# Last token block of a bilinear transformer layer: how the down stages are dealt between the products

## The chip, the cores and the metric

The kernel runs on one of the eight cores of a Trainium2 chip. The core's engines run side by side and meet at semaphores: TensorE (PE in the profile; its weight loads, PEld, overlap its matmuls), VectorE (DVE), ScalarE (ACT), GpSimd (POOL) and SyncE (SP), which here issues the transfers between memory and the on-chip buffers. The metric is the device time of one execution in microseconds (us); lower is better.

## The reference

One pre-norm layer on 2048 tokens of width 576: attention with 32 query heads of 18 and one shared key and value head, then a feed-forward part without a nonlinearity, the product of two projections to 4608, brought back by a third.

```python
h  = x + attention(layernorm(x)) @ wo          # 32 heads, one k and one v
xn = layernorm(h)
g  = xn @ w_gate                               # 576 -> 4608
u  = xn @ w_up                                 # 576 -> 4608
out = h + (g * u) @ w_down                     # 4608 -> 576
```

All is float32, and the change touches the last part of the feed-forward alone.

## The kernel before

The tokens are worked in four blocks of 512 (`TB`, `NB`). Blocks 0 to 2 have attention work mixed into their feed-forward. The last block (`b = 3`) has none left and is worked by `last_block`. The 4608 hidden columns are 18 pairs (`NC`, loop variable `p`) of 256. A float32 matrix product is made of three matmuls, high by high, high by low and low by high, of operands that were split before: ScalarE casts the high part (`high`), VectorE subtracts it to get the low part (`low`).

**Products.** For each pair, gate and up come from a seven-product scheme (the Winograd form of Strassen's) instead of eight: `product(i)` with i = 7p to 7p + 6 is 12 matmuls of 256 columns, and four of the seven are followed by a `tail` of 4 matmuls for the last 64 input columns. The results lie in four banks of the accumulator memory: `a` (`gs0` or `gs1`, by turns over the pairs), `b_` (`gs2`) and `c` (`gs3`). The bank `a` takes products 0, 3, 5 and 6 of a pair, and between two of them something must have read it: after product 5 that is VectorE's sum `gu22`. GpSimd multiplies gate by up (`both_halves`), giving the quarters a11, a21, a22 of the hidden tile; the last one, a12, comes from product 6 through ScalarE (`g`) and VectorE. Quarters and their sums S are split into an operand tile A with seven places. There are three such tiles in rotation (`AB`; one lies in the tile called `room`, two in the one called `XW`).

**Down stages.** The way back to 576 columns, `down_pairs`, takes two pairs at a time, also by seven products (`QUAD`). It is a generator of 14 steps: for each of the seven down weights (`wdo`, 288 KB each, from the `wd_dram` tensor, ten buffers) a step for each half t of 128 tokens. A step is three matmuls of 288 columns for each of the pairs, so six, into one half of the tile `yq` of that t (two banks), and then an add of that half to the residual h: on VectorE (L1112), or for four of the 14 steps (`ASIDE`) by a ScalarE copy (L1116) and a GpSimd add (L1117). The step of the second t also starts the loads of the next down weights. `last_block` takes steps of the generator D between the products by `go()`. While pairs 2 and 3 are multiplied, D holds pairs 0 and 1, and so on; while pairs 0 and 1 are multiplied, D holds the last pair of the block before, whose `down` has a plain form (L855): eight steps of six matmuls, one per token quarter s and half n of the columns, added by VectorE (n = 0) or by ScalarE and GpSimd (n = 1), and a store of the output rows after each s.

In the kernel before a pair takes seven steps: one after products 0, 1, 2, 3 and 6, two after product 5, none after product 4. So pairs 14 and 15 end after product 6 of pair 17, and behind it come pair 16 alone (14 steps of three matmuls) and pair 17 (eight plain groups of six, L1269, the first four into the banks `gs0`, `gs2`, `gs3`, `gs1`, the last four into two tiles `ye`, each used twice in a row), with an add (L1273) per group and a store of 288 KB per token quarter.

**Order.** The order on each engine is the order in which the code is written: no scheduler moves anything. An engine waits where its instruction's operand is not ready, and everything behind it on that engine waits too. `feed(i)` follows each product with the work for later ones: the low part of product i + 3's weights on VectorE, the high part of i + 4's on ScalarE, the load for i + 8 on SyncE.

Of the kernel before, what the change touches and what calls it, by code (L numbers as in the profile page):

```python
# [26 lines left out]
P = 128  # L27
S, D, H, DH, F = 2048, 576, 32, 18, 4608
TB = 512
NB = S // TB  # L30
# [4 lines left out]
NC = NF // 2  # L35
HT = TB // 2
HD = D // 2
# [20 lines left out]
class Block:  # L58
# [784 lines left out]
    def down(self, b, pair):  # L843

        pe, dve, act, sp, pool = self.pe, self.dve, self.act, self.sp, self.nc.gpsimd
        h = self.h[b]
        W = [self.wdo.pop((b, pair, j), None) for j in range(7)]
        if pair == NC - 1:
            ys = {}

            def part(s, n, i):

                ms = [(self.A[:, k, 2 * i + s // 2], W[(1, 0, 2, 3)[2 * i + n]][:, l]) for k, l in ((0, 0), (0, 1), (1, 0))]
                for j, (m, k) in enumerate(ms):
                    pe.matmul(ys[s, n][:, :HD], m[:, s % 2 * P:(s % 2 + 1) * P], k, start=(i == j == 0), stop=(i == 1 and j == 2))  # L855

            def add(s, n):
                hs, y = h[:, s, n * HD:(n + 1) * HD], ys.pop((s, n))[:, :HD]
                if n:
                    z = self.tmp[:, self.n_tmp % 5]  # L860
                    self.n_tmp += 1
                    act.copy(z, y)
                    pool.tensor_tensor(hs, hs, z, ALU.add)
                else:
                    dve.tensor_tensor(hs, hs, y, ALU.add)

            for s in range(NQ):
                if b == NB - 2:
                    e = self.ps_s(f"y{b}_{pair}_{s}")
                for n in range(2):  # L870
                    ys[s, n] = e[:, n] if b == NB - 2 else self.ps_y(2 * s + n, f"y{b}_{pair}_{s}_{n}")
                    part(s, n, 0)
                    part(s, n, 1)
                    add(s, n)
                    yield
                sp.dma_start(self.out[b * TB + s * P: b * TB + (s + 1) * P, :], h[:, s, :])
            return
        c, a = self.ps_f(f"y{b}_{pair}_2"), self.ps_f(f"y{b}_{pair}_0")
        banks = [a, self.ps_m(f"y{b}_{pair}_1"), c]
        for i, (t, bank, (x, w), first, (s, n), on_dve) in enumerate(STAGES):  # L880
            y = banks[bank]
# [6 lines left out]
            hs = h[:, t + 2 * s, n * HD:(n + 1) * HD]  # L888
# [234 lines left out]
    def last_block(self, ahead, D):  # L1123

        pe, act, dve, pool = self.pe, self.act, self.dve, self.nc.gpsimd
        b = NB - 1
# [25 lines left out]
        def both_halves(to, gu):  # L1152
            pool.tensor_tensor(to, gu[:, 0:HT], gu[:, HT:], ALU.mult)
# [7 lines left out]
        def low(i, src, n=1):  # L1161
            dve.tensor_tensor(A[:, 1, i:i + n], wide(src), f32(A[:, 0, i:i + n]), ALU.subtract)

        def go(n=1):
            for _ in range(n):
                next(D, None)

        late = []
        for p in range(NC):
            end = p == NC - 1  # L1170
            A = self.AB[(p + 1) % 3]
            if p % 2 == 0 and p:
                drain(D)
                D = self.down_pairs(b, (p - 2, p - 1))
# [4 lines left out]

            product(i, a, True)  # L1180
            act.copy(c1, a)
            go()
# [6 lines left out]
            go()  # L1189
# [5 lines left out]
            go()  # L1195
# [5 lines left out]
            go()  # L1201
# [5 lines left out]
            both_halves(a21, gu12)  # L1207
            self.feed(i + 4)

            product(i + 5, a)  # L1210
# [9 lines left out]
            go(2)  # L1220
            if p == 1:
                drain(D)
                if self.n_wd < len(self.wd_list):
# [4 lines left out]
            tail(1, 2, a)  # L1228
            if end:
                high(5, a22)  # L1230
                go()
                low(5, a22)
            else:
                low(5, S[:, 2])
                dve.tensor_tensor(S[:, 0], a21, a22, ALU.add)
                high(2, a22)
                dve.tensor_tensor(S[:, 1], S[:, 0], a11, ALU.subtract)
                go()
                high(3, S[:, 0:2], 2)
                low(2, a22)  # L1240
            self.feed(i + 6)
# [13 lines left out]
                low(6, S[:, 3])  # L1255
            del hf, a11, a21, a12, a22, g
        drain(D)
        drain(self.down_pairs(b, (NC - 2,)))
        W = [self.wdo.pop((b, NC - 1, j)) for j in range(4)]
        k = 0  # L1260
        for s in (2, 3, 0, 1):
            for n in range(2):
                if k in (4, 6):
                    e = self.ps_s(f"ye{k}")
                y = (gs[0], b_, c, gs[1])[k] if k < 4 else e[:, k % 2]
                for x in range(2):
                    at = ((0, 4), (6, 5))[x][s // 2]
                    for j, (m, l) in enumerate(((0, 0), (0, 1), (1, 0))):
                        pe.matmul(y[:, :HD], A[:, m, at, s % 2 * P:(s % 2 + 1) * P], W[(1, 0, 2, 3)[2 * x + n]][:, l],  # L1269
                                  start=(x == j == 0), stop=(x == 1 and j == 2))  # L1270
                k += 1
                hs = h[:, s, n * HD:(n + 1) * HD]
                dve.tensor_tensor(hs, hs, y[:, :HD], ALU.add)  # L1273
            self.sp.dma_start(self.out[b * TB + s * P: b * TB + (s + 1) * P, :], h[:, s, :])

    def load_x(self, b):
        h = self.h[b] = self.hp.tile([P, NQ, D], F32, tag="h", name=f"h{b}")
# [88 lines left out]
    def run(self):  # L1366
# [160 lines left out]
def drain(gen):  # L1527
    for _ in gen:
        pass
# [85 lines left out]
```

## Time and profile before

| | us |
|---|---|
| median of 3 runs (2296.19 to 2300.3) | 2297.45 |
| the profiled execution | 2295.16 |
| its span, first to last instruction | 2293.4 |
| TensorE busy in it | 2252.8 |
| stage of pair 16 behind the products | 10.9 |
| stage of pair 17 behind it | 8.3 |

The last block begins near 1957 us and its last product ends at 2269.55. In rows of the profile the name before the arrow is the tile written, those behind it are the tiles read, with partitions x elements. A row of the timeline begins with the start and the length in us, ends with the number of instructions merged into it, and in square brackets with how long the engine had stood idle before and who released it. PEld rows are the better clock of TensorE's pace, since the ends of matmuls are modelled.

### The profile page before, as it was taken

What the parts mean: (1) busy time and instruction counts of PE and PEld (TensorE: products, weight loads), DVE (VectorE), ACT (ScalarE), POOL (GpSimd) and SP (SyncE); (2) the same over time, 40 slices, a digit from 0 to 9 for tenths busy, and PEclk for the clock granted to TensorE, in tenths of its full rate; (3) what the DMA queues carried; (4) which work ended last, traced back from release to release, by engine and by line L of the source; (5) the groups of instructions that cost most, each with busy time, mean ns of one, the idle gap of its engine ahead of it and who ended that gap; (6) DMA issues with size and microseconds to landing.
All of it is one profiled execution on the core that took longest, in us unless ns stands there. A gap on an engine that the chain in (4) does not pass through costs nothing.

```text
span 2293.4 us, 46345 instructions
## 1 busy us (share of the span) xinstructions
PE 2252.8 (98%) x17958; PEld 1631.7 (71%) x17958; DVE 1268.2 (55%) x2209; ACT 1509.5 (66%) x2046; POOL 713.0 (31%) x826
## 2 busy tenths in 40 slices
PE   7999999999999999999999999999999999999998
PEld 5333335777677777777777777777777788999998
DVE  7555635444445446444545445444444477788786
ACT  6888877767676765767776766577676623555553
POOL 5445401333233333323333333322222233222222
PEclk9999999999999999999999999999999999999999
DMA  5779843555455555644455554644343345677774
GB/s 173 247 255 300 285 167 97 168 156 161 153 171 167 168 171 155 211 143 162 155 175 161 170 172 157 212 146 130 125 130 107 121 154 161 209 241 235 242 239 149
DMA packets 199127, 407.05 MB, mean 177 GB/s; under 512 B 21326, under 2 KB 52942, under 8 KB 198902
## 3 DMA queue, kind: packets, MB, share of 16 engines
q1 hardware_dynamic: 196165, 392.78, 53.3%
q0 software_dynamic: 2736, 11.26, 1.6%
q8 instruction: 143, 2.34, 0.4%
q14 instruction: 83, 0.67, 0.1%
HBM read 317.27 MB, written 74.55 MB: 171 GB/s over the span
## 4 chain that ended last, share of the span: by engine, by line
PE 83%; DVE 3%; ACT 1%; issue 0%; DMA 0%; SPq 0%; DVEq 0%; ACTq 0%
PE pg L932 21%; PE acc L611 15%; PE y L884 13%; PE s L606 9%; PE gs L1143 8%; PE pu L932 5%; PE yq L1108 4%; PE yo L736 3%; PE gu L932 2%; PE gs L1150 2%; PE y L855 1%; ACT P L607 0%; DVE hf L961 0%; DVE ws L93 0%; ACT room L92 0%
## 5 line engine op out<-in xcount | busy, mean ns | idle before, releaser
L607 ACT ACTIVATE P<-s 128x1024 f32<-128x1024 f32 x1024 | 1026.2, 1027 | 280.9 <-PE s L606 199.6
L932 PE MATMUL pu<-X,ws 64*128 64x512 f32 x2565 | 693.4, 389 | 0.0
L932 PE MATMUL pg<-X,ws 64*128 64x512 f32 x2565 | 692.8, 389 | 0.0
L932 PEld LDWEIGHTS pg<-X,ws 64*128 64x128 f32 x2565 | 475.3, 185 | 67.5 <-DMA wsum<-in_wgs_dram 0.8
L611 PE MATMUL acc<-P,V 128*32 128x512 f32 x4096 | 491.3, 599 | 0.7 <-ACT P L607 0.6
L932 PEld LDWEIGHTS pu<-X,ws 64*128 64x128 f32 x2565 | 472.6, 185 | 11.5
L606 PE MATMUL s<-q,kT 56*128 56x512 f32 x2048 | 438.5, 422 | 6.0 <-ACT P L607 3.1
L895 POOL TENSOR_TENSOR h<-h,tmp 128x288 f32<-128x288 f32 x306 | 238.7, 808 | 613.6 <-ACT tmp L894 612.6
L606 PEld LDWEIGHTS s<-q,kT 56*128 56x128 f32 x2048 | 197.2, 184 | 206.6 <-ACT P L607 120.5
L884 PEld LDWEIGHTS y<-wdo,room 128*128 128x128 f32 x2142 | 289.5, 188 | 45.1 <-issue 34.5
L884 PE MATMUL y<-wdo,room 128*128 128x288 f32 x2142 | 303.0, 300 | 3.6 <-DVE h L890 3.6
L611 PEld LDWEIGHTS acc<-P,V 128*32 128x32 f32 x4096 | 114.5, 109 | 247.2 <-issue 240.1
L890 DVE TENSOR_TENSOR h<-h,y 128x288 f32<-128x288 f32 x408 | 176.1, 453 | 199.3 <-PE y L884 199.1
L894 ACT COPY tmp<-y 128x288 f32<-128x288 f32 x306 | 122.3, 400 | 240.7 <-PE y L884 224.4
L961 DVE TENSOR_TENSOR hf<-pu,g 128x512 f32<-128x512 f32 x95 | 65.8, 692 | 301.7 <-ACT g L957 300.4
L92 POOL CAST ws<-wr 128x1152 fp32r<-128x1152 f32 x108 | 126.3, 1170 | 324.4 <-PE pu L932 235.1
L93 DVE TENSOR_TENSOR ws<-wr,ws 128x1152 fp32r<-128x1152 f32 x108 | 182.5, 1690 | 62.6 <-POOL ws L92 62.6
L1091 POOL TENSOR_TENSOR wsum<-wsum,wsum 128x512 f32<-128x512 f32 x72 | 99.0, 1376 | 139.9 <-DMA wsum<-in_wgs_dram 139.9
L93 DVE TENSOR_TENSOR room<-S,room 128x1024 fp32r<-128x1024 f32 x51 | 62.7, 1229 | 133.9 <-ACT room L92 133.9
L1108 PE MATMUL yq<-wdo,XW 128*128 128x288 f32 x504 | 88.2, 302 | 1.9 <-DVE h L1112 1.5
L737 DVE TENSOR_TENSOR h<-h,yo 128x288 f32<-128x288 f32 x160 | 65.1, 452 | 33.3 <-PE yo L736 33.2
L932 PE MATMUL gu<-X,ws 64*128 64x512 f32 x702 | 81.9, 389 | 0.0
(245 smaller groups left out, 2622.1 us busy)
## 6 DMA issues: line engine op xcount, KB each, us to landing
wdo<-wd_dram SPq DMA_DIRECT2D x492, 288.0 KB
wr<-in_wgu_dram SPq DMA_DIRECT2D x108, 576.0 KB
wsum<-in_wgs_dram SPq DMA_DIRECT2D x108, 256.0 KB
wd_dram<-wd_room SPq DMA_DIRECT2D x20, 1008.0 KB
wsum_dram<-wsum SPq DMA_DIRECT2D x72, 256.0 KB
raw<-wsum_dram SPq DMA_DIRECT2D x72, 256.0 KB
q<-q_dram SPq DMA_DIRECT2D x64, 216.0 KB
raw<-in_wgs_dram SPq DMA_DIRECT2D x54, 256.0 KB
```

The source lines that it names most:

```text
L92: (copy or self.cast)(hi, src)
L93: self.dve.tensor_tensor(lo, src, f32(hi), ALU.subtract)
L606: self.pe.matmul(s_[:, i], self.kT[o:o + 56, t * P:(t + 1) * P], q[o:o + 56, pr], start=True, stop=True)
L607: self.act.activation(p_, s_, AF.Exp, scale=SCALE)
L611: self.pe.matmul(acc[32 * j:32 * j + 32, :], self.V[:, t, :], Ps[j // 2][:, j % 2, :], start=(t == 0), stop=(t == NT - 1), skip_group_chec ...
L884: pe.matmul(y[:, :HD], m[:, t * P:(t + 1) * P], k, start=(first and j == 0), stop=(j == 2), skip_group_check=True)
L890: dve.tensor_tensor(hs, hs, y[:, :HD], ALU.add)
L894: act.copy(z, y[:, :HD])
L895: pool.tensor_tensor(hs, hs, z, ALU.add)
L932: pe.matmul(ps, w[o:o + 64, wk, c], X[o:o + 64, xk, c], start=(j == 0), stop=(j == 26))
L1108: pe.matmul(y[:, :HD], A[:, k, x, t * P:(t + 1) * P], v[:, l], start=(first and z == j == 0), stop=(z == len(pairs) - 1 and j == 2), skip_ ...
L1143: pe.matmul(bank[:, g * HT:(g + 1) * HT], W[:, wk, c, g], X[:, 2 * xk + c], start=(first and g == c == wk == xk == 0), stop=(c == 1 and wk ...
```

## The change

Four things change in the code.

The number of steps after each product is now read from a table, `DEALT`: a row for pairs 0 and 1, one for pairs 2 to 15 (as before, seven a pair), one for pairs 16 and 17. In pairs 16 and 17 it is two after every product. Pair 16 thus takes all 14 steps of pairs 14 and 15, and pair 17 all 14 steps of pair 16, whose generator is now made at the start of pair 17. Behind the products only pair 17's eight groups are left. In pairs 0 and 1 it is one step after products 1, 2, 3 and 5.

The plain steps of pairs 0 and 1 use two tiles made once, one for each half n of the columns, in place of one tile for each s; the half of the tile is s mod 2. Likewise the last four groups go by turns to two `ye` tiles.

The last token quarter is stored in two halves of its columns, the first as soon as it is added.

```diff
+            if b == NB - 2:
+                e = [self.ps_s(f"y{b}_{pair}_{n}") for n in range(2)]
             for s in range(NQ):
-                if b == NB - 2:
-                    e = self.ps_s(f"y{b}_{pair}_{s}")
                 for n in range(2):
-                    ys[s, n] = e[:, n] if b == NB - 2 else self.ps_y(2 * s + n, f"y{b}_{pair}_{s}_{n}")
+                    ys[s, n] = e[n][:, s % 2] if b == NB - 2 else self.ps_y(2 * s + n, f"y{b}_{pair}_{s}_{n}")
...
-        def go(n=1):
-            for _ in range(n):
+        def go(k):
+            for _ in range(DEALT[0 if p < 2 else 2 if p > NC - 3 else 1][k]):
                 next(D, None)
...
-            if p % 2 == 0 and p:
+            if p % 2 == 0 and p or end:
                 drain(D)
-                D = self.down_pairs(b, (p - 2, p - 1))
+                D = self.down_pairs(b, (p - 1,) if end else (p - 2, p - 1))
...
         drain(D)
-        drain(self.down_pairs(b, (NC - 2,)))
         W = [self.wdo.pop((b, NC - 1, j)) for j in range(4)]
         k = 0
         for s in (2, 3, 0, 1):
             for n in range(2):
-                if k in (4, 6):
-                    e = self.ps_s(f"ye{k}")
-                y = (gs[0], b_, c, gs[1])[k] if k < 4 else e[:, k % 2]
+                if k == 4:
+                    e = [self.ps_s(f"ye{x}") for x in range(2)]
+                y = (gs[0], b_, c, gs[1])[k] if k < 4 else e[k % 2][:, k // 2 - 2]
...
-            self.sp.dma_start(self.out[b * TB + s * P: b * TB + (s + 1) * P, :], h[:, s, :])
+                if s == 1:
+                    self.sp.dma_start(self.out[b * TB + s * P: b * TB + (s + 1) * P, n * HD:(n + 1) * HD], hs)
+            if s != 1:
+                self.sp.dma_start(self.out[b * TB + s * P: b * TB + (s + 1) * P, :], h[:, s, :])
...
+DEALT = [(0, 1, 1, 1, 0, 1, 0), (1, 1, 1, 1, 0, 2, 1), (2, 2, 2, 2, 2, 2, 2)]
```

In the listings that follow, a row is one group of instructions in the order of its engine: the line, the operation, the tile written and the tiles read, the shape, the count. In `wdo_16_3` the numbers are the pair and the weight; the long number behind a name tells copies of a tile apart.

TensorE at the end of the last product, before: rows L1143 and L1150 are products and tails, L1108 a down step's matmuls.

```order
L1108 MATMUL yq_0_32465<-wdo_14_1_32556,room 128x288 x3
L1108 MATMUL yq_0_32465<-wdo_15_1_32558,XW 128x288 x3
L1143 MATMUL gs_28983<-kT,wss 128x256 x12
L1150 MATMUL gs_28983<-XT_d,wt 128x256 x4
L1108 MATMUL yq_1_32466<-wdo_14_1_32556,room 128x288 x3
L1108 MATMUL yq_1_32466<-wdo_15_1_32558,XW 128x288 x3
L1108 MATMUL yq_0_32864<-wdo_16_0_32620,XW 128x288 x3
L1108 MATMUL yq_1_32865<-wdo_16_0_32620,XW 128x288 x3
L1108 MATMUL yq_0_32864<-wdo_16_3_32622,XW 128x288 x3
```

The same place now:

```order
L1143 MATMUL gs_28983<-kT,wss 128x256 x12
L1150 MATMUL gs_28983<-XT_t,wt 128x256 x4
L1108 MATMUL yq_0_32748<-wdo_16_6_32633,XW 128x288 x3
L1108 MATMUL yq_1_32749<-wdo_16_6_32633,XW 128x288 x3
L1143 MATMUL gs_28983<-kT,wss 128x256 x12
L1150 MATMUL gs_28983<-XT_d,wt 128x256 x4
L1108 MATMUL yq_0_32748<-wdo_16_1_32674,XW 128x288 x3
L1108 MATMUL yq_1_32749<-wdo_16_1_32674,XW 128x288 x3
L1269 MATMUL gs_28982<-wdo_17_1_32716,room 128x288 x3
L1269 MATMUL gs_28982<-wdo_17_2_32718,room 128x288 x3
```

Pair 16's steps stand between the products, six matmuls after each; twelve of the 14 steps that stood behind the last product stand ahead of it, and pair 17's first group follows the other two.

VectorE at that place, before. L1212 is `gu22`, L1162 a low part (into `room`, the operand tile of pair 17), L1246 the quarter a12, L1112 the adds of the down steps.

```order
L1212 TENSOR_TENSOR gu_28981<-gs_28983,cs 128x512
L1162 TENSOR_TENSOR room<-hfl_0_32668,room 128x256
L1112 TENSOR_TENSOR h_23390<-h_23390,yq_0_32465 128x288
L1112 TENSOR_TENSOR h_23390<-h_23390,yq_1_32466 128x288
L1162 TENSOR_TENSOR room<-hfl_1_32669,room 128x256
L1246 TENSOR_TENSOR hfl_1_32669<-gs_28983,gl_32859 128x256
L1162 TENSOR_TENSOR room<-hfl_1_32669,room 128x256
L1112 TENSOR_TENSOR h_23390<-h_23390,yq_0_32864 128x288 x2
```

And now:

```order
L1213 TENSOR_TENSOR gu_28981<-gs_28983,cs 128x512
L1162 TENSOR_TENSOR room<-hfl_0_32733,room 128x256
L1112 TENSOR_TENSOR h_23390<-h_23390,yq_0_32748 128x288 x2
L1112 TENSOR_TENSOR h_23390<-h_23390,yq_1_32749 128x288
L1162 TENSOR_TENSOR room<-hfl_1_32734,room 128x256
L1247 TENSOR_TENSOR hfl_1_32734<-gs_28983,gl_32921 128x256
L1162 TENSOR_TENSOR room<-hfl_1_32734,room 128x256
L1273 TENSOR_TENSOR h_23390<-h_23390,gs_28982 128x288
```

The low part of a22 (the second L1162) stands behind three adds where it stood behind two, and the groups of pair 17 are the next to be added after a12's low part.

TensorE in pair 0, before: L855 are the plain steps.

```order
L855 MATMUL y_17_0_29001<-wdo_17_1_28662,room 128x288 x3
L855 MATMUL y_17_0_29001<-wdo_17_2_28664,room 128x288 x3
L1143 MATMUL gs_28985<-XS_28303,wrs_28913 128x256 x12
L1150 MATMUL gs_28985<-XT_t,wt 128x256 x4
L855 MATMUL y_17_0_29001<-wdo_17_0_28660,room 128x288 x3
L855 MATMUL y_17_0_29001<-wdo_17_3_28879,room 128x288 x3
L1143 MATMUL gs_28984<-XS_28304,room 128x256 x12
```

And now:

```order
L1143 MATMUL gs_28985<-XS_28303,wrs_28913 128x256 x12
L1150 MATMUL gs_28985<-XT_t,wt 128x256 x4
L855 MATMUL y_17_0_29022<-wdo_17_1_28662,room 128x288 x3
L855 MATMUL y_17_0_29022<-wdo_17_2_28664,room 128x288 x3
L1143 MATMUL gs_28984<-XS_28304,room 128x256 x12
L855 MATMUL y_17_1_29023<-wdo_17_0_28660,room 128x288 x3
L855 MATMUL y_17_1_29023<-wdo_17_3_28879,room 128x288 x3
```

The first step moved from behind product 0 to behind product 1 with its tail, and the second step writes another tile than the first.

More of the change, by code (lines that the diff above doesn't have):

```diff
@@ L1181, in last_block @@
             act.copy(c1, a)
-            go()
+            go(0)
             self.feed(i)
@@ L1188, in last_block @@
             both_halves(a11, gu11)
-            go()
+            go(1)
             self.feed(i + 1)
@@ L1194, in last_block @@
             high(0, a11)
-            go()
+            go(2)
             low(0, a11)
@@ L1200, in last_block @@
             act.copy(c2, a)
-            go()
+            go(3)
             self.feed(i + 3)
@@ L1207, in last_block @@
             both_halves(a21, gu12)
+            go(4)
             self.feed(i + 4)
@@ L1219, in last_block @@
                 high(5, S[:, 2])
-            go(2)
+            go(5)
             if p == 1:
@@ L1230, in last_block @@
                 high(5, a22)
-                go()
+                go(6)
                 low(5, a22)
@@ L1237, in last_block @@
                 dve.tensor_tensor(S[:, 1], S[:, 0], a11, ALU.subtract)
-                go()
+                go(6)
                 high(3, S[:, 0:2], 2)
```

## The prediction

> **What bounds the kernel now.** I read the head of the page first, for the share of TensorE, and then cut the last block into stages with windows, to see in which of them TensorE is not full.
>
> ```profile
> span 2293.4 us, 46345 instructions
> PE 2252.8 (98%) x17958; PEld 1631.7 (71%) x17958; DVE 1268.2 (55%) x2209; ACT 1509.5 (66%) x2046; POOL 713.0 (31%) x826
> ```
>
> TensorE is busy for 2252.8 of 2293.4 us, so 40.6 us is all that waits can give back, and the change neither adds nor removes a matmul. What it can win must stand in the stages that it touches. In the windows the columns are: the window, its length, then busy time (and instructions) of PE, PEld, DVE, ACT and POOL, then the granted clock, the DMA share and GB/s.
>
> ```profile
> 2235.20:2252.80 17.60, 17.60 (x144) 17.60 (x143) 14.76 (x29) 9.38 (x20) 4.68 (x5) 1.00 0.78 244
> 2252.80:2269.55 16.75, 16.75 (x139) 16.75 (x138) 10.92 (x23) 7.37 (x16) 4.10 (x5) 1.00 0.42 133
> 2270.30:2281.20 10.90, 8.98 (x45) 7.23 (x43) 5.47 (x13) 1.91 (x5) 2.68 (x4) 0.84 0.27 81
> 2281.20:2289.50 8.30, 7.21 (x51) 6.53 (x49) 3.68 (x9) 0.00 (x0) 0.52 (x1) 1.00 0.28 109
> 2289.50:2293.40 3.90, 0.03 (x1) 0.00 (x0) 0.46 (x1) 0.00 (x0) 0.00 (x0) 0.75 0.19 76
> ```
>
> The first two rows are pairs 16 and 17 with their products and dealt steps: TensorE has no gap at all. The third is pair 16's own down stage behind the products (42 matmuls), the fourth the last pair's (48), the fifth the last store. The weight loads, one per matmul and not pipelined like the matmuls' modelled ends, show the gaps best: 7.23 of 10.90 and 6.53 of 8.30. The list of waits of this tail (waited in total, times, longest) says for whom:
>
> ```profile
> PEld yq L1108 <- DVE h L1112: 3.4, 7, 1.5
> PEld ye L1269 <- DVE h L1273: 1.6, 2, 0.8
> ```
>
> TensorE waits for the VectorE add that reads the other half of the same two-bank tile (yq, ye). Between two products such an add has 1.5 us or more of other matmuls to run under; behind the products it has 0.39 us.
>
> **Pair 16's stage goes between the products.** What would the 42 matmuls cost with no wait? From the weight loads of the timeline (start, length, count):
>
> ```profile
> 2266.03 0.44 PEld L1108 LDWEIGHTS yq<-wdo,room 128*128 128x128 f32 x3
> 2266.81 0.45 PEld L1108 LDWEIGHTS yq<-wdo,room 128*128 128x128 f32 x3
> 2267.62 1.52 PEld L1143 LDWEIGHTS gs<-kT,wss 128*128 128x128 f32 x12
> 2269.55 0.45 PEld L1108 LDWEIGHTS yq<-wdo,room 128*128 128x128 f32 x3
> 2273.20 0.82 PEld L1108 LDWEIGHTS yq<-wdo,XW 128*128 128x128 f32 x6 [1.50 <-DVE h L1112]
> 2276.04 1.46 PEld L1108 LDWEIGHTS yq<-wdo,XW 128*128 128x128 f32 x6 [0.17 <-DVE h L1112]
> ```
>
> Six matmuls are 2266.81 - 2266.03 = 0.78 us apart, so 0.13 us each, 42 are 5.46 us, and the stage takes 10.90: the gain is **5.4 us**. (A product with its tail is 2269.55 - 2267.62 = 1.93 us for 16 matmuls, one without a tail 12/16 of that, 1.45.) The other moves there are even: pairs 14 and 15 give seven more six-matmul steps to pair 16 (5.5 us) and take them from pair 17, which gets fourteen three-matmul steps in their place (also 5.5 us). Bounds: if a third of the waiting came along it would be 4.0; the stage cannot cost less than its matmuls, so 5.5 is the top.
>
> Part of the 10.90 is the clock, not the waits:
>
> ```profile
> 1976.20:1993.00 16.80, 16.02 (x133) 15.81 (x132) 14.04 (x27) 10.11 (x22) 3.82 (x4) 1.00 0.66 203
> 2270.30:2274.40 4.10, 2.48 (x15) 1.77 (x13) 2.40 (x7) 0.70 (x2) 0.79 (x1) 1.00 0.68 198
> 2274.40:2277.80 3.40, 3.39 (x13) 3.04 (x13) 1.33 (x3) 0.40 (x1) 0.80 (x1) 0.50 0.06 22
> ```
>
> After 4.10 us with loads in only 1.77 of them, the granted clock is 0.50 for 3.40 us, and six loads take 1.46 instead of 0.82 us. The 13 loads of that window took 3.04 us, against 13 x 0.137 = 1.78: 1.3 us lost, which is inside the 5.4. In the window of 1976 a single wait of 1 us left the clock at 1.00. The Trainium skill ("TensorE: Matmul & The Clock Gate", section "Part 1: The HAM clock gate") says that the clock halves after at least one idle window of about 3.4 us. The trace agrees on the length and the half, and not on the condition, since the longest wait here was 1.50 us. Read literally, that rule would have kept the gate open here, the stage would have been 1.3 us shorter and the whole gain below 1.3 us smaller; the row decides. In the changed tail I expect no wait beyond 0.6 us in any 3.4 (82% loaded), so no halving.
>
> **The last pair's ye tiles.** The k-th product alternates now between two tiles instead of going twice to one.
>
> ```profile
> 2281.20 3.25 PEld L1269 LDWEIGHTS gs<-wdo,room 128*128 128x128 f32 x24
> 2284.40 0.85 PEld L1269 LDWEIGHTS ye<-wdo,room 128*128 128x128 f32 x6
> 2285.52 0.46 DVE L1273 TENSOR_TENSOR h<-h,ye 128x288 f32<-128x288 f32 x1 [0.34 <-PE ye L1269]
> 2286.03 1.65 PEld L1269 LDWEIGHTS ye<-wdo,room 128*128 128x128 f32 x12 [0.78 <-DVE h L1273]
> 2288.46 0.83 PEld L1269 LDWEIGHTS ye<-wdo,room 128*128 128x128 f32 x6 [0.78 <-DVE h L1273]
> ```
>
> A group starts at 2284.40 and its add ends at 2285.98, 1.58 us later; one other group of 0.79 us would then hide all but 0.05 us of it (the second group's start is 0.79 after the first, the third's 1.58). Two waits of 0.78 become two of at most 0.1: **+1.4 us** (1.2 to 1.56).
>
> **What is late next.** With pair 16 gone from behind the products, nothing covers the last pair's own preparation. Its first group's sixth matmul reads the low part of a22; the second half needs a12's.
>
> ```profile
> 2266.34 0.69 DVE L1212 TENSOR_TENSOR gu<-gs,cs 128x512 f32<-128x512 f32 x1 [1.14 <-PE gs L1150]
> 2270.76 0.45 DVE L1112 TENSOR_TENSOR h<-h,yq 128x288 f32<-128x288 f32 x1 [2.35 <-PE yq L1108]
> 2271.13 0.42 DVE L1162 TENSOR_TENSOR room<-hfl,room 128x256 fp32r<-128x256 f32 x1
> 2271.47 0.42 DVE L1246 TENSOR_TENSOR hfl<-gs,gl 128x256 f32<-128x256 f32 x1
> 2271.92 0.41 ACT L1159 CAST room<-hfl 128x256 fp32r<-128x256 f32 x1 [1.64 <-DVE hfl L1246]
> 2272.36 0.42 DVE L1162 TENSOR_TENSOR room<-hfl,room 128x256 fp32r<-128x256 f32 x1 [0.47 <-ACT room L1159]
> ```
>
> Take the end of the last product as T (2269.55 here). VectorE's queue then holds the adds of pair 16's last two steps (the second can start at T + 1.15: two steps of 0.39 and the 0.37 from issue to add), then low of a22 to T + 2.0, a12 to T + 2.4, ScalarE's cast to T + 2.8, low of a12 to T + 3.3. TensorE issues the two steps to T + 0.78, five matmuls to T + 1.43 and then waits to about T + 2.05: **-0.6 us** (0.2 to 1.3). The first four groups run to T + 5.2, so a12, ready at T + 3.3, is covered, and so is the bank of a12 (read by T + 2.4, written at T + 4).
>
> The sixth and seventh products share a bank, and gu (2266.34 to 2267.03, 1.0 us after the product's end at 2266.03) must be read between them. Four groups of three (1.57 us) covered that; in pair 17 two of 0.39 do: **-0.2 us** (0 to 0.3). In pair 16 it stays covered by 1.57.
>
> VectorE is also later at the border of pairs 16 and 17:
>
> ```profile
> 2252.14 0.57 PE L1108 MATMUL yq<-wdo,room 128*128 128x288 f32 x3
> 2253.37 0.45 DVE L1112 TENSOR_TENSOR h<-h,yq 128x288 f32<-128x288 f32 x1
> 2256.97 0.45 DVE L1112 TENSOR_TENSOR h<-h,yq 128x288 f32<-128x288 f32 x1
> ```
>
> The step behind pair 16's seventh product began at 2252.02 in loads (matmuls show 0.12 later); the add of pair 17's first step started 4.95 us after that, behind the splits. With one add more ahead of it, which itself waits for a step 0.78 us later, it starts about 0.7 later and ends at 6.1. Its tile is wanted again at 1.57 + 1.45 + 0.78 + 1.93 = 5.73 (two long steps, a product, two short steps, a product with its tail): **-0.4 us** (0 to 1.0). Elsewhere VectorE has room: pair 16 brings five more adds, 2.3 us, to a stage 5.5 us longer, and pair 17 brings five to 16.75 us of which 10.92 are used.
>
> **The first pairs.** Seven of the eight plain steps stood in pair 0 and one in pair 1; now it is four and four.
>
> ```profile
> 1959.11 0.30 PEld L855 LDWEIGHTS y<-wdo,room 128*128 128x128 f32 x2 [0.32 <-ACT room L92]
> 1959.84 0.19 PEld L855 LDWEIGHTS y<-wdo,room 128*128 128x128 f32 x1 [0.43 <-DVE room L93]
> 1972.63 0.82 PEld L855 LDWEIGHTS y<-wdo,room 128*128 128x128 f32 x6 [0.92 <-DVE h L865]
> 1987.95 1.48 PEld L1143 LDWEIGHTS gs<-kT,wss 128*128 128x128 f32 x12 [0.99 <-DVE gu L1212]
> ```
>
> The first step stands one product later and meets its operand ready: 0.75 saved. The two adjacent steps on one tile are separated: 0.92 saved. Pair 1's uncovered gu gets one step of 0.78 for its 0.99, and pair 0's keeps one instead of two: 0.99 becomes 0.2 + 0.2. In sum 2.66 - 0.4 = **+2.3 us** (1.5 to 2.7). SyncE issues the last of these output stores later, in front of four weight loads and one product's load; those loads are for products more than six ahead (over 12 us), which hides the 2 to 3 us.
>
> **The last store.**
>
> ```profile
> 2289.56 0.46 DVE L1273 TENSOR_TENSOR h<-h,ye 128x288 f32<-128x288 f32 x1 [1.15 <-PE ye L1269]
> 2283.70 6.68 SPq L1274 DMA_DIRECT2D out_dram<-h  x4
> GB/s 0 0 0 0 0 0 0 0 0 0 217 407 407 434 434 407 434 407 271 55 0 0 0 0 0 0 0 0 0 0 0 0 0 0 0 0 0 0 0 0
> ```
>
> The third row cuts 2290.0 to 2293.4 into slices of 0.085 us: the 288 KB move in about 0.75 us. Half of them go 0.8 us earlier, so the end comes 0.35 sooner: **+0.35 us** (-0.1, if the shorter rows move worse, to 0.4).
>
> **The sum**: 5.4 + 1.4 - 0.6 - 0.2 - 0.4 + 2.3 + 0.35 = 8.25 us; the worse ends together give 4.0 + 1.2 - 1.3 - 0.3 - 1.0 + 1.5 - 0.1 = 4.0, the better ones 5.5 + 1.56 - 0.2 + 2.7 + 0.4 = 10.0. The profiled execution took 2295.16 us (span 2293.4), 2.3 below the median of 2297.45, so 2286.9 for an execution like it and 2289.2 for the median.
>
> **Rivals.** A change below 0.2% (4.6 us) can hardly be told from none here.
> 1. The waits come along: in pairs 16 and 17 each yq tile is written again after one product instead of two. For it speaks the border above; against it that everywhere else an add has over 1.5 us. At 0.3 us for each of 13 places 3.9 us are lost: 2293.1.
> 2. The first pairs gain nothing, since their waits move to the next product: 2.3 lost, 2291.5.
> 3. The dealing of pair 16 does not do what it says, and its waits of 5.4 us go with it: 2294.6.
> 4. Slower: weight supply. Pair 16 now asks for 14 down weights of 288 KB instead of 8.
>
> ```profile
> DMA packets 2273, 4.41 MB, mean 245 GB/s; under 512 B 255, under 2 KB 255, under 8 KB 2270
> ```
>
> That row is 2235 to 2253; with six more (1.77 MB) it is 6.2 MB in 23.1 us, 268 GB/s. Ten weight buffers are filled ahead, and single slices of the trace exceed 400 GB/s, so I expect no wait. At the 245 of now, 2.2 us would be lost; slower than before by over 0.2% needs 13 us lost, which is 6.2 MB in 36 us or 172 GB/s: 2302 there, and the clock would halve in such gaps.
>
> **Chances.** My forecast 0.73, rival 1 0.12, rival 2 0.08, rival 3 0.04, rival 4 0.03. Faster by over 0.2%: the forecast, rival 2 and half of rival 1, 0.87; within 0.2%: the rest of rival 1 and rival 3, 0.10; slower 0.03. The range: the bounds of the sum give 2287.4 to 2293.4, and the runs before lie 1.3 below to 2.9 above their median, so 2286.0 to 2293.5, which takes in rivals 1 and 2.
>
> **What would show it.** Right: no stage of yq behind the last product but two steps, that is some 8.5 us from the last product's end to the last add (20.5 now), granted clock 1.00 in it; ye without a wait above 0.1; one wait near 0.6 for the low part of a22; waits near 0.2 for gu in pairs 0, 1 and 17; windows of pair 16 full. Wrong: PEld waits on h inside pairs 16 and 17, or a wait for wdo, or a window at clock 0.50.

## The result and the profile after

Changed, the kernel takes 2289.39 us (median of 10 runs, 2288.55 to 2292.91) against 2297.28 for the kernel before (10 runs, 2294.7 to 2300.3): a ratio of 0.9968, 95% interval 0.9959 to 0.9977, so 7.4 us or 5.3 to 9.4. A second comparison of the same two kernels gave 0.9964 (0.9951 to 0.9978). The forecast was 2289.2 us, 8.25 us below.

The head of the page, the same windows as before (pair 16 with its products, pair 17 with its products, what lies behind the last product; the fourth is pairs 0 and 1) and the list of TensorE's waits in the last block:

```profile
span 2287.4 us, 46347 instructions
PE 2249.7 (98%) x17958; PEld 1624.3 (71%) x17958; DVE 1271.1 (56%) x2209; ACT 1508.0 (66%) x2046; POOL 714.7 (31%) x826
```

```profile
2234.50:2258.25 23.75, 23.75 (x190) 23.63 (x189) 17.56 (x35) 10.04 (x22) 5.90 (x7) 1.00 0.83 275
2258.25:2275.91 17.66, 17.54 (x141) 17.13 (x140) 12.89 (x27) 7.97 (x18) 6.37 (x7) 1.00 0.21 68
2275.91:2284.00 8.09, 7.76 (x57) 7.29 (x55) 5.02 (x13) 0.78 (x2) 0.00 (x0) 1.00 0.23 90
1959.20:1991.28 32.08, 32.08 (x262) 31.61 (x261) 25.16 (x42) 17.27 (x37) 9.73 (x10) 1.00 0.49 158
```

```profile
PEld gs L1143 <- DVE gu L1213: 0.7, 3, 0.2
PEld gs L1269 <- DVE room L1162: 0.5, 1, 0.5
PEld yq L1108 <- ACT tmp L1116: 0.3, 1, 0.3
```

The number of matmuls is the same (17958). The reader is to see that the two long entries of before, 3.4 us on the shared yq tile and 1.6 us on ye, are gone, that pair 16 with fourteen six-matmul steps fills its window and is fed at 275 GB/s, and that the clock is 1.00 in all four rows. What remains are five named waits of 1.5 us in sum. The timeline of the weight loads behind the last product (start, length, count) shows what is left there:

```profile
2275.91 0.84 PEld L1108 LDWEIGHTS yq<-wdo,XW 128*128 128x128 f32 x6
2276.69 0.72 PEld L1269 LDWEIGHTS gs<-wdo,room 128*128 128x128 f32 x5
2277.93 2.58 PEld L1269 LDWEIGHTS gs<-wdo,room 128*128 128x128 f32 x19 [0.52 <-DVE room L1162]
2280.46 3.25 PEld L1269 LDWEIGHTS ye<-wdo,room 128*128 128x128 f32 x24
```

The last two down steps of pair 16 take 0.78 us, five matmuls of the last pair follow, the sixth waits 0.52 for the low part of a22, and the ye groups run through without a gap.

The last block can be cut at four events that both kernels have: its first product, the first down step of pair 2, the end of the last product, the last add, and then the end of the span. This table, worked out from the starts of the weight loads, the end of the last add and the end of the span of each profile (2293.37 and 2287.45 us to the hundredth), is the measure for all experiments below:

| profile | first product at | to pair 2's first down step | to the last product's end | to the last add | to the end |
|---|---|---|---|---|---|
| before | 1956.92 | 34.36 | 278.27 | 20.47 | 3.35 |
| after | 1959.22 | 32.06 | 284.63 | 8.53 | 3.01 |
| difference | +2.30 | -2.30 | +6.36 | -11.94 | -0.34 |

From the first product on the change gains 2.30 - 6.36 + 11.94 + 0.34 = 8.22 us. The spans differ by 5.92 only, because this execution reached the first product 2.30 us later, in code that is the same in both kernels; whether that belongs to the change is tested below.

### The profile page after: what moved, and what is told of

The parts are those of the page before. It is cut to its first block, busy times and chain, and to the rows that moved or that the text cites. A ratio compares the mean times of both kernels' runs of the same rounds, so it can differ in the third digit from the quotient of the medians.

```text
span 2287.4 us, 46347 instructions
## 1 busy us (share of the span) xinstructions
PE 2249.7 (98%) x17958; PEld 1624.3 (71%) x17958; DVE 1271.1 (56%) x2209; ACT 1508.0 (66%) x2046; POOL 714.7 (31%) x826
## 4 chain that ended last, share of the span: by engine, by line
PE 82%; DVE 3%; ACT 1%; DMA 1%; issue 0%; SPq 0%; ACTq 0%; DVEq 0%
PE pg L932 20%; PE acc L611 15%; PE y L884 13%; PE s L606 9%; PE gs L1143 8%; PE pu L932 5%; PE yq L1108 4%; PE yo L736 2%; PE gu L932 2%; PE gs L1150 2%; PE y L855 1%; ACT P L607 1%; DVE room L93 0%; DVE hf L961 0%; DVE ws L93 0%
## 5 line engine op out<-in xcount | busy, mean ns | idle before, releaser
L1108 PE MATMUL yq<-wdo,XW 128*128 128x288 f32 x504 | 86.0, 297 | 0.1
```

The source lines that it names most:

```text
L1108: pe.matmul(y[:, :HD], A[:, k, x, t * P:(t + 1) * P], v[:, l], start=(first and z == j == 0), stop=(z == len(pairs) - 1 and j == 2), skip_ ...
```

## The experiments

Nine runs, on chips that also ran the kernel before. The medians of single parts lie within a few us of one another, so each verdict rests on the cuts of the table above; the ratios stand beside them.

### One part at a time

**The first pairs alone.** The kernel before with the two tiles by n and one step behind products 1, 2, 3 and 5 in pairs 0 and 1:

```diff
+            if b == NB - 2:
+                e = [self.ps_s(f"y{b}_{pair}_{n}") for n in range(2)]
...
+DEALT = [(0, 1, 1, 1, 0, 1, 0), (1, 1, 1, 1, 0, 2, 1), (1, 1, 1, 1, 0, 2, 1)]
```

> Kernel before with the first pairs alone changed: four plain steps in pair 0 and four in pair 1, on two tiles by turns; the rest as before. My theory: it gives 2.3 us of the whole (from the first product of the last block to pair 2's first down step 32.1 us instead of 34.4), with two waits of about 0.2 us for gu and none for the plain steps' tile or operand. Rival: the first pairs' waits only move on to a later product, and the stretch stays above 34 us.

Measured: ratio 0.9984 (0.9976 to 0.9993). Pair 2's first down step begins 32.06 us after the first product, 2.30 less than before and the same as in the changed kernel. The rest of the block is as before (278.31 to the last product's end, 3.36 from the last add to the end), but for the clock: here the stage behind the products, with the same 3.4 us of waiting in seven places, stayed at full clock.

```profile
PEld yq L1108 <- DVE h L1112: 3.4, 7, 1.5
PEld gs L1143 <- DVE gu L1213: 0.4, 2, 0.2
```

```profile
2271.40:2277.50 6.10, 4.38 (x26) 3.42 (x25) 3.33 (x9) 1.12 (x4) 1.12 (x2) 1.00 0.48 145
2277.50:2281.20 3.70, 3.54 (x20) 2.56 (x19) 1.95 (x5) 0.80 (x2) 1.51 (x3) 1.00 0.00 0
```

From the end of the last product to the last pair's first group it took 10.56 us, against 11.65 in the kernel before. So the waits do not always halve the clock, and in the profile of the kernel before it cost some 1.1 us of this stage.

**The dealing in pairs 16 and 17 alone.**

```diff
-            if p % 2 == 0 and p:
+            if p % 2 == 0 and p or end:
                 drain(D)
-                D = self.down_pairs(b, (p - 2, p - 1))
+                D = self.down_pairs(b, (p - 1,) if end else (p - 2, p - 1))
...
-        drain(self.down_pairs(b, (NC - 2,)))
...
+DEALT = [(1, 1, 1, 1, 0, 2, 1), (1, 1, 1, 1, 0, 2, 1), (2, 2, 2, 2, 2, 2, 2)]
```

> Kernel before with the dealing in pairs 16 and 17 alone changed (two steps after each product, pair 16's stage in pair 17); the first pairs, the ye tiles and the last store as before. My theory: from the last product's end to the last add 20.5 us become 20.5 - 10.9 + 0.8 (the last two steps) + 0.5 (wait for the low part of a22) = about 10.4, pairs 16 and 17 get 6.4 us longer (5.5 of moved matmuls, 0.9 of waits for gu and at the border), so about 4 us gained in all, 2293.2 to 2293.6; the granted clock is 1.00 behind the products. Rival: the two-bank tiles make the steps wait between the products too, so that pairs 16 and 17 grow by 9 us or more and the gain is below 1.5 us.

Measured: ratio 0.9979 (0.9971 to 0.9988). 34.41 us to pair 2's first down step, 284.67 to the last product's end (6.4 more than before), 10.12 from there to the last add (10.35 less). Its waits in the last two pairs are those of the changed kernel, with the two on ye still there:

```profile
PEld ye L1269 <- DVE h L1273: 1.6, 2, 0.8
PEld gs L1143 <- DVE gu L1213: 1.2, 2, 1.0
PEld gs L1269 <- DVE room L1162: 0.5, 1, 0.5
```

(The 1.2 for gu is the old 1.0 of pair 1 and the new 0.2 of pair 17.) This part alone gains 3.9 us, and all the small new waits of the end come with it.

**The ye tiles by turns and the last store in halves alone.**

```diff
-                if k in (4, 6):
-                    e = self.ps_s(f"ye{k}")
-                y = (gs[0], b_, c, gs[1])[k] if k < 4 else e[:, k % 2]
+                if k == 4:
+                    e = [self.ps_s(f"ye{x}") for x in range(2)]
+                y = (gs[0], b_, c, gs[1])[k] if k < 4 else e[k % 2][:, k // 2 - 2]
...
+                if s == 1:
+                    self.sp.dma_start(self.out[b * TB + s * P: b * TB + (s + 1) * P, n * HD:(n + 1) * HD], hs)
```

> Kernel before with only the last four groups on two ye tiles by turns and the last store in two halves; all down stages where they were. My theory: the two ye waits of 0.78 us go (at most 0.1 each left), and from the last add to the end 3.4 us become 3.0: 1.8 us in all. Pair 16's stage stays 10.9 us with its 3.4 us at clock 0.50. Rival: the ye groups wait for VectorE anyhow, since each add follows its group by 0.8 us, and only the store's 0.4 is won.

Measured: ratio 0.9988 (0.9979 to 0.9997). The two waits on ye are gone (24 loads in one row, below), and from the last add to the end it is 3.01 us instead of 3.35. From the last product's end to the last add it is 18.65, 1.8 less than before, of which 1.6 are the two waits and 0.2 a half clock that cost less. That clock was halved again for 3.41 us of pair 16's stage (the third number from the end of the second row):

```profile
2291.11 3.26 PEld L1269 LDWEIGHTS ye<-wdo,room 128*128 128x128 f32 x24
```

```profile
2280.49:2283.90 3.41, 3.41 (x15) 3.08 (x14) 1.36 (x3) 0.40 (x1) 0.05 (x1) 0.50 0.21 74
```

The three parts gain 2.30, 3.9 and about 1.9 us (1.6 for ye and 0.3 for the store) by their cuts: 8.1, against 8.22 for the whole. So within 0.1 us they do not help or hinder one another.

### What makes the waits behind the products

The prediction said that TensorE waits for the add that reads the other half of the same two-bank tile. The rival was that VectorE is simply too slow for a step every 0.39 us. To tell them apart, pair 16 stays behind the products as before, but its steps go to four tiles of one bank each:

```diff
-                y = banks[t][:, bank]
+                y = spare[t] if spare and bank else banks[t][:, bank]
...
-        drain(self.down_pairs(b, (NC - 2,)))
+        drain(self.down_pairs(b, (NC - 2,), (gs[0], c)))
```

> Kernel before with pair 16's stage where it was, behind the products, but its four sums in four separate tiles (two halves of yq, and gs0 and gs3), so that a step no longer waits for the add of the other half of its own tile; the last pair's first four groups use the same four banks in another order. Theory A (the shared two-bank tile makes the waits): the stage falls from 10.9 to 7.5 to 8 us (5.5 of matmuls, 1.4 at its start while VectorE makes the last operands, 0.8 at the last two steps), the clock stays at 1.00, gain about 3 us. Theory B (what costs is the place behind the products, where the adds queue behind VectorE's other work and each other): the stage stays above 9.5 us, gain under 1.5 us, and the clock halves again.

Measured: ratio 0.9987 (0.9978 to 0.9995). The waits on yq fall from 3.4 us in seven places to 1.1 in two:

```profile
PEld yq L1108 <- DVE h L1112: 1.1, 2, 0.7
```

The stage takes 8.13 - 0.78 = 7.35 us behind the last step of pairs 14 and 15, where the kernel before took 11.65 - 0.78 = 10.87. With the clock whole in this run, some 1.1 of those 3.5 us are the clock's; against the first pairs' run, whose clock was whole too (10.56 - 0.78 = 9.78), 2.4 are left for the tile. So the shared tile was the main cause. Of what is left (7.35 against 5.46 for the bare matmuls) the waits name VectorE with 1.1 us, which has the splits of the last quarters to do at the same time, and ScalarE's copy with 0.3. That last wait is not one of a shared tile: in `QUAD` the fifth and the sixth weights go to the same half, so it stays with four tiles. Separate tiles alone thus would have kept a third of the waiting; the dealing takes all of it but 0.5 us at two borders between pairs (below).

### The spread between executions

**The changed kernel once more**, without an edit.

> The changed kernel once more, unedited, for its spread from execution to execution. Theory A: what differs between profiled executions lies ahead of the last block, in the granted clock of the first 100 us (six profiles so far: first product of the last block at 1956.9 to 1960.3 with a clock of 1.00 there, 1961.8 to 1962.0 with 0.98, 1963.7 with 0.95); then the stretches of the last block repeat to 0.2 us (32.06, 284.63, 8.53, 2.96 us) whatever the total is. Theory B: the 2.3 us by which the first profile of this kernel reached the last block later than the kernel before belongs to the change; then the first product stands again at 1959.2 or later with a clock of 1.00.

Measured: 2288.29 us (5 runs, 2287.76 to 2293.32), ratio 0.9964. The profile's first product stands at 1957.63, and the cuts are 32.05, 284.70, 8.55 and 3.00 us: none differs from the first profile by more than 0.07. The 2.30 us by which the first profile came late to the last block thus are no part of the change.

**The kernel before once more**, without an edit.

> The kernel before once more, unedited, to see whether the half clock of 3.4 us in pair 16's stage behind the products belongs to the kernel. If it does, the stage takes 10.9 us again and its loads read double for 3.4 us. If, as the profile of the kernel with only the first pairs' part suggests (clock 1.00 in a stage with the same waits), it depends on the execution, either 10.9 with the half clock or some 9.7 without, and the rest (34.36 us to pair 2's first down step, 278.3 to the last product's end) as before.

Measured: first product at 1959.74, then 34.39, 278.32, 20.18 and 3.35 us. The stage behind the products takes 11.37 - 0.78 = 10.59 us, with a half clock again, later in the stage than in the first profile:

```profile
2277.67:2281.08 3.41, 3.41 (x15) 3.03 (x13) 1.42 (x4) 0.40 (x1) 0.80 (x1) 0.50 0.00 0
```

In four profiles in which this stage has its 3 us of waiting (both of before, the first pairs alone, ye alone) the clock fell in three, each time to 0.50 for one piece of 3.41 us; with four tiles and 1.1 us of waiting it stayed at 1.00. By these two kernels' second profiles the spans are 2296.0 and 2285.9, 10.1 apart; by the first ones 5.9. The mean of the two is 8.0, beside 7.9 and 8.2 by the medians. By the cuts the change gains 8.22 in the first two profiles and 7.94 in the second two (336.24 and 328.30 us from the first product to the end); the difference lies mostly in the half clock, which cost 0.8 in place of 1.1.

Where the spread sits is seen in a stretch that no part of the change touches, the start of the program. The window of the first 100 us in the first profile of the kernel before (its last block began at 1956.92) and in the run with the latest first product of all (the last experiment below, 1966.16); the granted clock is the third number from the end:

```profile
0.00:100.00 100.00, 83.19 (x517) 44.80 (x517) 68.86 (x144) 70.91 (x83) 49.51 (x103) 1.00 0.61 201
```

```profile
0.00:100.00 100.00, 82.19 (x462) 44.58 (x464) 64.75 (x135) 64.56 (x76) 45.83 (x98) 0.93 0.57 186
```

With the mean clock of the first 100 us the first product of the last block moves: 1956.9 to 1960.3 in five profiles at 1.00, 1959.7 to 1962.0 in four at 0.98, 1963.7 at 0.95 and 1966.2 at 0.93. The means hide that the clock falls there, too, to 0.50 for whole pieces of 3.41 us, one or several. In the run at 0.93 these are:

```profile
50.61:54.02 3.41, 3.41 (x11) 1.94 (x9) 2.27 (x4) 0.84 (x2) 0.44 (x1) 0.50 0.71 179
57.44:67.68 10.24, 10.02 (x37) 3.46 (x39) 5.69 (x8) 4.64 (x6) 6.81 (x7) 0.50 0.54 140
```

Half of their 13.65 us, 6.8 us, is the most that TensorE can have lost by them, of the 9.2 us by which this run is later than the first. What makes the clock fall there in one execution and not in another is left open, and so is the spread of 3.4 us among those at 1.00.

### Is the weight supply near its limit?

**The weights wanted sooner.** The slower rival was that pair 16 would run out of down weights. Here pair 16 takes its fourteen steps (4,4,4,2,0,0,0) instead of two a product:

```diff
-            for _ in range(DEALT[0 if p < 2 else 2 if p > NC - 3 else 1][k]):
+            for _ in range(DEALT[0 if p < 2 else 2 if p == NC - 2 else 3 if end else 1][k]):
...
-DEALT = [(0, 1, 1, 1, 0, 1, 0), (1, 1, 1, 1, 0, 2, 1), (2, 2, 2, 2, 2, 2, 2)]
+DEALT = [(0, 1, 1, 1, 0, 1, 0), (1, 1, 1, 1, 0, 2, 1), (4, 4, 4, 2, 0, 0, 0), (2, 2, 2, 2, 2, 2, 2)]
```

> The changed kernel with pair 16's fourteen steps dealt (4,4,4,2,0,0,0), so that the last of its fourteen down weights is wanted some 4.7 us earlier: the same bytes in about 18 us instead of 23. It tests the rival of the weight supply. Theory A, that ten buffers filled ahead and a queue with room cover it: no wait for wdo, the rate in pair 16's first 18 us rises to 320 GB/s or more; what is lost is the wait for gu before the seventh product (1.0 us, nothing stands before it now) and waits for the yq tile inside each group of four steps (0.3 to 0.8 a group), 2 to 4 us in all over the changed kernel. Theory B, that the supply of the weights is at its limit at the 275 GB/s of the changed kernel: the rate stays at 275 and TensorE waits for wdo, up to 4.7 us.

Measured: one time of 2291.36 us; 32.05, 288.43, 8.50 and 3.00 us, so 3.8 us more than the changed kernel, all of it before the last product's end. There is no wait for wdo. The waits, and the window of the fourteen steps:

```profile
PEld yq L1108 <- DVE h L1112: 2.1, 1, 2.1
PEld gs L1143 <- DVE gu L1213: 1.7, 4, 1.0
PEld yq L1108 <- ACT tmp L1116: 1.0, 1, 1.0
PEld gs L1269 <- DVE room L1162: 0.5, 1, 0.5
```

```profile
2233.70:2253.33 19.63, 17.80 (x139) 17.55 (x137) 11.46 (x25) 7.79 (x18) 3.95 (x5) 1.00 0.81 256
```

Two things were expected wrongly. The rate did not rise to 320 GB/s, it was 256, since the bytes are not the same: in the shorter stretch fewer weights of products are loaded, so that it moves 5.03 MB where the 23.75 us of the changed kernel move 6.54. So neither theory's rate came, and the verdict rests on the missing wait: pair 16's last down weights were taken 18.0 us after its first product began, where the changed kernel takes them after 21.8. That is 3.8 us sooner (the wait of 2.1 us below took the rest of the 4.7), and supply still costs nothing. And within the groups of four the tiles cost nothing after the first group, where 0.3 to 0.8 each was expected. A six-matmul step is 0.78 us, and that is enough cover for an add that starts 0.33 after the step (2239.97 after 2239.64) and takes 0.45; the three-matmul steps of 0.39 that stood behind the products are not. The 2.1 us come at the border, where VectorE does the splits of pair 15 before the first add; the 1.0 on `tmp` is the wait at the next border, between pairs 16 and 17. The longest wait for gu, 1.0, is the one expected before pair 16's seventh product.

### Can the small new waits be ordered away?

**All of them at once.** The changed kernel with three moves in the order:

```diff
-                go(6)
                 low(5, a22)
+                go(6)
...
-DEALT = [(0, 1, 1, 1, 0, 1, 0), (1, 1, 1, 1, 0, 2, 1), (2, 2, 2, 2, 2, 2, 2)]
+DEALT = [(0, 1, 1, 0, 0, 2, 0), (1, 1, 1, 1, 0, 2, 1), (1, 2, 2, 2, 2, 3, 2)]
```

> The changed kernel with its four small new waits taken out by order alone: pairs 0 and 1 deal their four steps (0,1,1,0,0,2,0), so that two stand before the seventh product; pairs 16 and 17 deal (1,2,2,2,2,3,2), so that three stand there; and the low part of a22 is split before the two adds of the seventh product instead of behind them. My theory, that these waits are what is left of the change's losses and that each goes when its cover or its order is given back: no wait for gu in pairs 0, 1 and 17 (0.22, 0.23 and 0.23 in the changed kernel), none for the low part of a22 (0.52), the borders of pairs 15/16 and 16/17 (0.20 and 0.30) gone or smaller since one add less is queued there. From the first product of the last block to pair 2's first down step 31.6 us (32.06 after), to the last product's end 283.9 (284.63), from there to the last add 8.0 (8.53): 1.3 to 1.7 us below the changed kernel in these stretches, a ratio to it of 0.9993, less than the times of few runs can tell. The rival, that the waits only move on to the next bank that VectorE has not read: the same 325.2 us in sum, with new waits for gu, h or room of the same total in those places.

Measured: 2289.82 us (5 runs), ratio to the kernel before 0.9963 (0.995 to 0.9977). The cuts are 31.62, 285.49, 7.99 and 3.00. The first and the third are as expected: the waits for gu in pairs 0 and 1 and that for a22 are gone. The middle is 0.86 longer instead of 0.7 shorter, because of the third step in a row of pair 17:

```profile
2274.80 0.83 PEld L1108 LDWEIGHTS yq<-wdo,XW 128*128 128x128 f32 x6
2275.11 0.69 DVE L1213 TENSOR_TENSOR gu<-gs,cs 128x512 f32<-128x512 f32 x1 [1.57 <-PE gs L1150]
2275.72 0.42 DVE L1162 TENSOR_TENSOR room<-hfl,room 128x256 fp32r<-128x256 f32 x1
2276.05 0.81 DVE L1112 TENSOR_TENSOR h<-h,yq 128x288 f32<-128x288 f32 x2
2276.55 0.43 PEld L1108 LDWEIGHTS yq<-wdo,XW 128*128 128x128 f32 x3 [0.93 <-DVE h L1112]
```

The third step is the twelfth of the generator and goes to the very half that the tenth wrote (the fifth and the sixth weights share it). The tenth's add is the first of the two in the row of 2276.05, and it stands behind gu and a low part in VectorE's order. So three short steps behind one product bring a wait back, here not by the other half of a shared tile but by the same half and by what stands ahead of its add. In sum 325.10 us from the first product to the last add, against 325.22: in the last pairs the rival was right, the waits moved on.

**Only the two that held.** The same, with pairs 16 and 17 dealt two a product again:

```diff
-DEALT = [(0, 1, 1, 0, 0, 2, 0), (1, 1, 1, 1, 0, 2, 1), (1, 2, 2, 2, 2, 3, 2)]
+DEALT = [(0, 1, 1, 0, 0, 2, 0), (1, 1, 1, 1, 0, 2, 1), (2, 2, 2, 2, 2, 2, 2)]
```

> The changed kernel with the two reorderings that kept their gain in the run before (pairs 0 and 1 dealt (0,1,1,0,0,2,0), the low part of a22 split before the seventh product's adds) and with pairs 16 and 17 dealt two a product again, where three steps behind one product had cost 0.93. If the pieces add up: 31.6 us to pair 2's first down step, 284.6 from there to the last product's end, 8.0 to the last add, 3.0 to the end: 324.25 us from the last block's first product to the last add against 325.2 in the changed kernel, with waits of 0.2 to 0.3 at the two borders and for gu in pair 17 only. If the earlier split of a22 moves pair 17's waits, the middle stretch grows by up to 0.5 and the sum stays near 325. The times will hardly tell it from the changed kernel (0.04%): ratio to the kernel before 0.996.

Measured: 2289.73 us (6 runs, 2286.57 to 2295.24), ratio to the kernel before 0.9965 (0.9953 to 0.9977). The cuts are 31.61, 284.67, 7.99 and 3.01: 324.27 us from the first product to the last add, as expected, and 0.95 less than the changed kernel.

```profile
PEld yq L1108 <- ACT tmp L1116: 0.3, 1, 0.3
PEld gs L1143 <- DVE gu L1213: 0.2, 1, 0.2
```

```profile
2282.44 0.84 PEld L1108 LDWEIGHTS yq<-wdo,XW 128*128 128x128 f32 x6
2283.22 3.27 PEld L1269 LDWEIGHTS gs<-wdo,room 128*128 128x128 f32 x24
2286.43 3.28 PEld L1269 LDWEIGHTS ye<-wdo,room 128*128 128x128 f32 x24
```

Behind the last product TensorE now never waits. By the trace this is the best version; by the times it can't be told from the changed kernel, since 0.95 us is less than its runs scatter.

## Why the prediction was right

The sum held to 0.03 us by the cuts of the first two profiles (8.25 predicted, 8.22 measured), to 0.3 by those of the second two, and the time to 0.2 us. Its terms, by its own steps:

| step | predicted | measured | from |
|---|---|---|---|
| pair 16's stage goes between the products | +5.4 | +5.41 | 10.87 of the stage, 5.46 for its matmuls |
| ye by turns | +1.4 | +1.59 | both waits gone altogether |
| wait for the low part of a22 | -0.6 | -0.52 | the row of 2277.93 |
| gu in pair 17 | -0.2 | -0.23 | one of three in 0.7 |
| border of pairs 16 and 17 | -0.4 | -0.30 | the wait of yq |
| first pairs | +2.3 | +2.30 | 34.36 to 32.06 |
| last store in halves | +0.35 | +0.34 | 3.35 to 3.01 |
| not named | 0 | -0.37 | the rest of the cuts |

The mechanism held term by term, each within 0.2 us. That the sum agrees to 0.03 is luck: the ye tiles, the low part of a22 and the border of pairs 16 and 17 came out 0.37 us better than predicted in sum, and 0.37 of losses had not been named.

The stage's 5.4 was right in size and, as predicted, not all of it was waiting. The share of the half clock was put at 1.3 us; the stage without it (10.56 against 11.65 in the first pairs' run) says 1.1, in those executions that have it. An execution of the kernel before without the half clock leaves the change about 7.1 us to gain instead of 8.2.

What was to be wrong did not come: behind the last product the clock is 1.00 (the window of 2275.91), no load waits for h between the products of the last two pairs but at the two borders (0.20 and 0.30 us, told below), and none waits for wdo.

The step on ye was 0.19 too careful: it left up to 0.1 us of each of the two waits, and there is none.

The border of pairs 16 and 17 came where it was expected, with 0.30 us in place of 0.4. The record names ScalarE's copy as the releaser, which ends at 2263.08, while VectorE's add of the same tile's neighbour ends at 2263.12 and the load starts at 2263.19:

```profile
2263.19 0.82 PEld L1108 LDWEIGHTS yq<-wdo,XW 128*128 128x128 f32 x6 [0.30 <-ACT tmp L1116]
```

The code says which of the two was awaited. This is the third step of its generator; it writes one half of the tile of t = 0, and the other half is read by the first step's add. That add is VectorE's, while `ASIDE` gives ScalarE the second step, in the tile of t = 1. So the wait is for VectorE's add, as predicted, and not for the copy that the row names. What the prediction missed is the border before it: of the 0.37 us, 0.20 stand between pairs 15 and 16, where the third step's loads began at 2240.47, right behind the add that VectorE started at 2239.97, after four splits of pair 15. The remaining 0.17 is about what two six-matmul steps in a row cost more than two single ones: the seven such pairs of steps of pair 16 take 1.56 to 1.61 us each, 11.16 in sum, and fourteen times 0.78 is 10.92.

```profile
2239.62 0.42 DVE L1162 TENSOR_TENSOR XW<-S,XW 128x256 fp32r<-128x256 f32 x1
2239.97 0.45 DVE L1112 TENSOR_TENSOR h<-h,yq 128x288 f32<-128x288 f32 x1
2240.47 0.43 PEld L1108 LDWEIGHTS yq<-wdo,room 128*128 128x128 f32 x3
```

Rival 1, that the waits come along between the products, gave 0.3 us for each of 13 places, 3.9 us; measured are 0.50 us in two places (0.73 in three with gu in pair 17). It has a true core, which the last experiments show: three short steps in a row (0.93 us), or four long ones at a border (2.1), do bring waits along. Two a product were few enough here. Rivals 2 and 3 fell with the first and second run: each part gained what was laid to it alone. Rival 4, too little weight supply, fell by the changed kernel (275 GB/s and no wait, where 268 had been worked out as needed) and by the run that wanted the weights sooner.

## What to carry to other kernels

Work that stands alone at a kernel's end pays for every buffer hand-over in full; dealt between long products the same matmuls cost little but their own time, as long as no more short steps stand in a row than the reader of their shared tile can follow (0.78 us of cover per hand-over was enough here, 0.39 was not), and as long as that reader is not queued behind other work (0.93 and 2.1 us where VectorE's add was). Put what the very last step needs ahead of the adds that nothing waits for. And where executions scatter by more than an edit is worth, cut the trace at events that both versions share: here cuts of the same code repeated to 0.07 us, or to 0.3 where the clock fell, while the totals moved by several.

## What was not expected of the hardware

The granted clock fell to 0.50 in the stage with the waits in three of four profiles, each time for one piece of 3.41 us, which began 4.0 to 5.2 us after the last product's end (at 2274.39, 2277.67 and 2280.49). It did not fall at all in the first pairs' run with the same seven waits of 3.4 us. So the half clock here is a matter of the execution as well as of the code, and it was worth 0.8 to 1.1 us of the stage (10.56 us with the clock whole, 11.37 to 11.65 without). The Trainium skill ("TensorE: Matmul & The Clock Gate", section "Part 1: The HAM clock gate") says that the gate's window of about 3.4 us runs freely and does not start with the kernel, so that its transitions differ from run to run. The profiles agree with that difference and with the length. They do not agree that a whole window has to be idle, the condition in the prediction's words from the same section, since the longest wait in any of them was 1.50 us.

The start of the program does the same on a larger scale, in pieces of the same 3.41 us or of several of them. A mean granted clock between 0.93 and 1.00 in the first 100 us goes with a first product of the last block anywhere from 1956.9 to 1966.2, 9 us apart, more than the whole change gains.
